# Retention and squared-ReLU feed-forward: two more chunks in halves of 64 tokens, and the preparation for that form placed later

## The chip, the core and the metric

The kernel runs on one core of a Trainium2 chip. A core has TensorE (PE in the profile; its weight loads are PEld), VectorE (DVE), ScalarE (ACT), GpSimd (POOL) and a queue on SyncE (SP) from which this kernel issues all its DMAs. Each engine works through its own instructions in order and waits on semaphores for the others. The metric is device time in microseconds of the whole program. Before the change three runs gave 1238.62, 217.63 and 218.36 us, with 218.36 as the median.

## What is computed

For 4 batches of 8 heads, 768 tokens and 64 dimensions a decaying state is carried along the tokens; the result goes through a feed-forward layer with a squared ReLU.

```python
gamma = 1.0 - 2.0 ** (-5.0 - np.arange(H, dtype=np.float32))
for t in range(S):
    state = gamma[None, :, None, None] * state + np.einsum('bhd,bhe->bhde', k[:, :, t], v[:, :, t])
    y[:, :, t] = scale * np.einsum('bhd,bhde->bhe', q[:, :, t], state)
...
x = np.ascontiguousarray(attn_out.transpose(0, 2, 1, 3)).reshape(B * S, H * D)
h = np.maximum(x @ w_in, 0.0)
return (h * h @ w_out).astype(np.float32)
```

`x` is 3072 x 512, `w_in` 512 x 2048, `w_out` 2048 x 512; all arrays are float32. The kernel multiplies in bf16.

## The kernel before, in words

The tokens are cut into 24 chunks of 128, six to a batch. The decay is taken out by scaling: q is multiplied by a table `qf`, k by a table `kf`, and what is left for a chunk is ordinary masked attention inside it (`scores`: k times q, masked by `cmask` on VectorE; then times v) plus the product of q with the running state of the chunks before it (`state` adds k times v into one PSUM tile, `c_ps`, that lives for a whole batch; `outputs` adds both parts up and ScalarE copies them into `xt`, the feed-forward's input). Heads go in four pairs. A pair is put on the 128 rows of TensorE with zeros where one head's data would meet the other's, hence the block-diagonal tiles `k_bd`, `v_bd` and `s_bd`, whose zero parts are written once.

There are two forms. In the **wide form** (chunks 0 to 11) a chunk is one block of 128 tokens. Its keys are transposed and spread into `k_bd` (`spread_k`, two copies on VectorE, once the transpose is made by DMA), the scores are taken in two portions of two pairs, both through one PSUM tile `st` (`ps_st` has a single buffer), each masked by one instruction at line 394, and the state of a pair is 128 columns wide, of which each head uses its own 64. In the **halves form** (from chunk `PACK_FROM` = 12, functions with a 2 in their names) a chunk is two blocks of 64 tokens, u = 0 and 1, and a row block of 128 holds 64 tokens of each of a pair's two heads. `scale_k2` writes scaled keys block-diagonally (two VectorE instructions of 64 rows), `cast_v2` makes three copies of the values on GpSimd, all of a chunk's scores fit into `st` at once with one masking instruction, the state is renewed after each half (`state2`), and it is only 64 columns wide. This form needs tables and masks of its own (`pack_constants`: memsets and iotas on GpSimd, exponents on VectorE, an exponential on ScalarE) and tiles whose off-diagonal parts are zero (`zero_off_diagonal`, a VectorE memset per half of the tile: `ks_bd2s`, `v_bd2s` and the third of the three `s_bds`).

Loads differ too. A wide chunk's k and v come in one DMA each (`load`). For the halves form `group_loads` fetches three chunks at once, one DMA for each of 8 heads and for k and v, 16 in all, put singly among the other work.

The order of work on every engine is written out by hand. The feed-forward of a block of chunks (`BLOCKS`: 4, then 2 each) is cut into pieces, eight to a chunk, counted from 4 on; a piece is about 0.9 us of TensorE. In blocks 1 and 2 (pieces 33 to 64) eight pieces of the first product of a block's two chunks come before eight of the second. `put(n, f, ...)` places an attention step, a load or a preparation directly after piece n, in the order in which `put` was called; `take_squares` then squares on VectorE (line 584) what ScalarE's ReLU (line 613) has just written. Nothing reorders this afterwards, so a step that must wait holds up all that stands behind it in the same engine's queue.

Places that matter here: the casts of the last quarter of `w_in` after piece 10; scaling of q for chunk 4 after 18 and its transpose on TensorE after 20; `pack_constants` after 8 and the ten zeroing memsets after 10 to 19. For chunk 8 the two portions of scores stand after pieces 50 and 52; for chunk 9 the cast of its values (`v_bd`, waiting until chunk 7's outputs have used the tile) stands after 49, its spread copies after 55, its scores after 57 and 59. A chunk m in the halves form whose outputs stand after piece d has its `scale_k2` and `cast_v2` after d - 15, the DMA transpose of the keys after d - 13, `state2` after d - 6 and d - 3, scores after d - 5. Chunk 10 has d = 70, chunk 11 has 78.

Of the kernel before, what the change touches and what calls it, by code (L numbers as in the profile page):

```python
# [9 lines left out]
FP32 = mybir.dt.float32  # L10
# [3 lines left out]
AF = mybir.ActivationFunctionType  # L14
# [7 lines left out]
DMA_FROM = 8  # L22


PACK_FROM = 12

GROUP = 3


@with_exitstack  # L30
def kernel(
# [9 lines left out]
    nc = tc.nc  # L41
    P = nc.NUM_PARTITIONS

    B, H, S, D = q.shape
    DM, DFF = moe_w_in.shape
    C = 128
    NCH = S // C
    NPAIR = H // 2
# [6 lines left out]
    NCHUNK = len(chunks)  # L55
# [9 lines left out]
    grpool = ctx.enter_context(tc.tile_pool(name="grpool", bufs=2))  # L65
# [13 lines left out]
    ps_c = ctx.enter_context(tc.tile_pool(name="ps_c", bufs=1, space=bass.MemoryType.PSUM))  # L79
# [23 lines left out]
            load_q(m)  # L103
        load_kv(m)

    def group_loads(m):

        b, i = chunks[m]
        for name, src, to in (("kg", k, raw_k), ("vg", v, raw_v)):
            t = grpool.tile([P, 2 * GROUP, NPAIR, D], FP32, name=name)  # L110
            for h in range(H):
                p, hh = divmod(h, 2)
                rows = slice(64 * hh, 64 * (hh + 1))
                nc.sync.dma_start(
                    t[rows, :, p, :],
                    src[b, h, i * C : (i + GROUP) * C, :].rearrange("(w s) d -> s w d", s=64),
                )
                yield
            for j in range(GROUP):
                to[m + j] = t[:, 2 * j : 2 * j + 2].rearrange("s u p d -> s (u p) d")  # L120

    w_in_v = moe_w_in.rearrange("(cb p) f -> p cb f", p=P)
# [28 lines left out]
    halves = [slice(0, 64), slice(64, 128)]  # L151
# [75 lines left out]
    s_bds = [const.tile([P, NPAIR, 2, D], BF16, name=f"s_bd{j}") for j in range(3)]  # L227
    ks_bd2s = [const.tile([P, 2 * NPAIR, 2, D], BF16, name=f"ks_bdp{j}") for j in range(2)]

    v_bd2s = [t.rearrange("s p (c hh) d -> s (p c) hh d", hh=2) for t in v_bds[2:]]  # L230
# [170 lines left out]
    c_ps = [None]  # L401
# [27 lines left out]
    def xt_of(m):  # L429
        tb = block_of[m]  # L430
        if m == first[tb]:
            xts[tb] = xtpool.tile([P, NCB, BLOCKS[tb] * C], BF16, name="xt")
        return tb, (m - first[tb]) * C
# [61 lines left out]
    def half_of(qT, p, u):  # L495
        return qT[:, :, p, u * (C // 4) : (u + 1) * (C // 4)]
# [28 lines left out]
    def state2(m, u):  # L525

        b, i = chunks[m]
        a = at[m]
        if i == NCH - 1 and u == 1:
            return  # L530
        if i == 0 and u == 0:
            c_ps[0] = ps_c.tile([P, NPAIR, D], FP32, name="c_ps")
        c = c_ps[0]
        for p in range(NPAIR):
            nc.tensor.matmul(  # L535
                c[:, p, :],
                lhsT=a["ks"][:, u * NPAIR + p],
                rhs=a["v2"][:, u * NPAIR + p, :],
                start=(i == 0 and u == 0 and p == 0),
                stop=True,  # L540
                skip_group_check=True,
            )
        s_bd = s_bds[(2 * m + u) % 3]
        nc.scalar.activation(s_bd[halves[0], :, 0, :], c[halves[0]], AF.Copy)  # L544
        nc.vector.tensor_copy(s_bd[halves[1], :, 1, :], c[halves[1]])  # L545

    def outputs2(m):
        b, i = chunks[m]
        a = at.pop(m)
        tb, off = xt_of(m)  # L550
        y = ps_y.tile([P, NPAIR, 2, C // 2], FP32, name="y")
        for u in range(2):
            inter = i > 0 or u > 0
            for p in range(NPAIR):
                yv = half_of(y.rearrange("e p r s -> e r p s"), p, u)
                if inter:
                    nc.tensor.matmul(  # L557
                        yv,
                        lhsT=s_bds[(2 * m + u - 1) % 3][:, p],
                        rhs=half_of(a["qT"], p, u),  # L560
                        start=True,
                        stop=False,
                    )
                nc.tensor.matmul(  # L564
                    yv,
                    lhsT=a["v_bd"][:, u * NPAIR + p],
                    rhs=a["pt"][:, u * NPAIR + p, :].rearrange("s (r t) -> s r t", r=2),
                    start=not inter,
                    stop=True,
                )  # L570
        nc.scalar.activation(  # L571
            xts[tb][:, :, off : off + C].rearrange("e p (s r) -> e p r s", r=2),
            y[:],
            AF.Copy,
        )
# [178 lines left out]
    def put(place, what, *args):  # L754
        parts.setdefault(place, []).append((what, args))
# [6 lines left out]
    def attend(m, scaled, places):  # L762
        by_dma = m >= DMA_FROM
        attend_q(m, scaled, scaled if by_dma else places[0])
        put(places[0], scale_kv, m)
        if by_dma:
            put(places[0], dma_transpose_k, m)
        put(places[1], spread_k if by_dma else transpose_k, m)
        put(places[2], scores, m, 0)
        put(places[3], scores, m, 1)  # L770
        put(places[3], state, m)
        put(places[4], outputs, m)

    def attend2(m, d):
        attend_q(m, d - 17, d - 15)
        put(d - 15, scale_k2, m)
        put(d - 15, cast_v2, m)
        put(d - 13, transpose_k2, m)
        put(d - 6, state2, m, 0)
        put(d - 5, scores2, m)  # L780
        put(d - 3, state2, m, 1)
        put(d, outputs2, m)
# [12 lines left out]
    attend(5, None, (27, 29, 31, 33, 35))  # L795
    attend(6, 30, (33, 35, 37, 39, 42))
    attend(7, None, (40, 42, 44, 46, 49))
    put(8, pack_constants)
    for j, t in enumerate(ks_bd2s + v_bd2s):
        for hh in range(2):  # L800
            put(10 + 2 * j + hh, zero_off_diagonal, t, hh)
    for hh in range(2):
        put(18 + hh, zero_off_diagonal, s_bds[2], hh)


    done = [55, 62, 70] + [78 + 8 * j for j in range(13)]
    for m, place in ((8, 26), (9, 31), (10, 36)):
        put(place, load, m)
    for m, d in zip(range(8, NCHUNK), done):
        if m < PACK_FROM:  # L810
            attend(m, d - 15 if d < 70 else d - 16, (d - 13, d - 7, d - 5, d - 3, d))
        else:
            attend2(m, d)
        if m + 3 < PACK_FROM:
            put(d - 13, load, m + 3)
        elif m + 3 < NCHUNK and (m + 3) % 2 == 0:
            put(d - 13, load_q, m + 3)
    for m, place in zip(range(PACK_FROM, NCHUNK, GROUP), (43, 67, 92, 116)):
        loads = group_loads(m)
        for j in range(2 * H):  # L820
            put(place + 3 * j // 2, next, loads)
        put(place + 3 * H, next, loads, None)

    def before(n):
        for what, args in parts.pop(n, []):
# [40 lines left out]
```

## Time and profile before

| what | value |
|---|---|
| median of the three runs | 218.36 us |
| the profiled execution | 219.42 us |
| its span, first to last instruction | 217.65 us |
| mean granted TensorE clock | 1.000 |
| VectorE's squares, line 584 | 96 instructions, 44.0 us |
| zeroing memsets, line 295 | 10 instructions, 2.5 us |
| group loads, line 114 | 64 DMAs of 96 KB, median 2.9 and 2.8 us to landing |
| key transposes by DMA, line 492 | 12, median 3.2 us to landing |

The span lies inside the profiled execution's own time; 1.77 us lie around it. A row of a timeline gives the start in us from the span's start, the time taken, engine, line and operation, what is written from what, and in square brackets how long the engine stood idle before and what ended that. The ends of matmuls are modelled: each shows some 0.2 to 0.4 us although in a stream they start far closer together, so a busy TensorE is not one at its peak, and the spacing of starts says more than the duration.

### The profile page before, as it was taken

What the parts mean: (1) busy time and instruction counts of PE and PEld (TensorE: products, weight loads), DVE (VectorE), ACT (ScalarE), POOL (GpSimd) and SP (SyncE); (2) the same over time, 40 slices, a digit from 0 to 9 for tenths busy, and PEclk for the clock granted to TensorE, in tenths of its full rate; (3) what the DMA queues carried; (4) which work ended last, traced back from release to release, by engine and by line L of the source; (5) the groups of instructions that cost most, each with busy time, mean ns of one, the idle gap of its engine ahead of it and who ended that gap; (6) DMA issues with size and microseconds to landing.
All of it is one profiled execution on the core that took longest, in us unless ns stands there. A gap on an engine that the chain in (4) does not pass through costs nothing.

```text
span 217.7 us, 5060 instructions
## 1 busy us (share of the span) xinstructions
PE 208.9 (96%) x2039; PEld 144.6 (66%) x2039; DVE 132.7 (61%) x257; ACT 119.0 (55%) x219; POOL 48.2 (22%) x103
## 2 busy tenths in 40 slices
PE   6898998899999999999999999999999999999994
PEld 1566743455985895794795785785775875965853
DVE  5766679825566686298379388387396495550420
ACT  8564777346874572472483572581673663753631
POOL 3222763711101110107030331205221223000000
PEclk9999999999999999999999999999999999999999
DMA  6999999998873986569598599697997323301102
GB/s 168 279 257 365 410 375 291 318 258 232 255 181 77 245 206 126 165 170 192 151 210 163 164 232 169 166 204 167 155 217 176 99 50 99 96 3 48 48 3 96
DMA packets 94711, 39.65 MB, mean 182 GB/s; under 512 B 74592, under 2 KB 88160, under 8 KB 94688
## 3 DMA queue, kind: packets, MB, share of 16 engines
q1 hardware_dynamic: 94688, 39.33, 70.3%
q8 instruction: 16, 0.26, 0.5%
q14 instruction: 7, 0.06, 0.1%
HBM read 27.26 MB, written 6.29 MB: 154 GB/s over the span
## 4 chain that ended last, share of the span: by engine, by line
PE 82%; DVE 11%; ACT 3%; DMA 2%; issue 1%; DVEq 0%; ACTq 0%
PE psf L662 35%; PE psf L604 33%; DVE h L584 3%; DVE qs L300 2%; PE y L450 2%; PE st L387 2%; DMA qn<-in_q_dram 2%; PE st L508 1%; PE y L564 1%; PE y L557 1%; PE c_ps L535 1%; PE tp L333 1%; ACT h L613 1%; PE c_ps L413 1%; DVE pt L394 1%
## 5 line engine op out<-in xcount | busy, mean ns | idle before, releaser
L604 PE MATMUL psf<-xt,w_in_bf 128*128 128x256 bf16 (+2 forms) x880 | 91.4, 259 | 1.0 <-DVE w_in_bf L259 0.6
L662 PE MATMUL psf<-w_out_bf,h 128*128 128x512 bf16 (+2 forms) x400 | 89.8, 371 | 0.0
L604 PEld LDWEIGHTS <-w_in_bf 128*128 128x128 bf16 x880 | 71.5, 98 | 13.2 <-DVE w_in_bf L259 1.4
L613 ACT ACTIVATE h<-psf 128x512 bf16<-128x512 f32 x96 | 56.8, 596 | 23.0 <-PE psf L604 20.4
L662 PEld LDWEIGHTS <-h 128*128 128x128 bf16 x400 | 36.3, 98 | 34.9
L584 DVE TENSOR_TENSOR h<-h 128x512 bf16<-128x512 bf16 x96 | 44.0, 471 | 21.8 <-ACT h L613 20.8
L672 ACT ACTIVATE osb<-psf 128x512 f32<-128x512 f32 (+2 forms) x25 | 14.4, 580 | 27.1 <-PE psf L662 26.9
L545 DVE CAST s_bd<-c_ps 64x256 bf16<-64x256 f32 x22 | 9.4, 428 | 27.0 <-ACT s_bd L544 26.5
L394 DVE TENSOR_TENSOR pt<-st,cmask 128x512 bf16<-128x512 f32 x20 | 13.8, 692 | 18.4 <-PE st L387 18.1
L483 POOL CAST v<-vg 128x512 bf16<-128x512 f32 x12 | 7.7, 643 | 55.8 <-PE c_ps L535 22.5
L319 POOL CAST v_bd<-vn 128x512 bf16<-128x512 f32 x12 | 8.1, 671 | 52.2 <-PE y L450 33.0
L486 POOL CAST v_bd<-vg 64x512 bf16<-64x512 f32 x24 | 15.9, 662 | 16.6 <-PE y L564 15.9
L470 DVE TENSOR_TENSOR ks_bdp<-kg,kf 64x512 bf16<-64x512 f32 x24 | 18.4, 765 | 0.4
L300 DVE TENSOR_TENSOR qs<-qn,qf 128x1024 bf16<-128x1024 f32 x12 | 14.9, 1240 | 0.8 <-DMA qn<-in_q_dram 0.8
L571 ACT ACTIVATE xt<-y 128x512 bf16<-128x512 f32 x12 | 8.9, 743 | 9.6 <-PE y L564 9.6
L458 ACT ACTIVATE xt<-y 128x512 bf16<-128x512 f32 x12 | 9.0, 749 | 7.9 <-PE y L450 7.5
L544 ACT ACTIVATE s_bd<-c_ps 64x256 bf16<-64x256 f32 x22 | 8.1, 367 | 8.8 <-PE c_ps L535 8.8
L279 PE MATMUL psf<-ident 128*128 128x512 bf16 (+1 forms) x48 | 8.9, 328 | 2.1 <-POOL ident L178 2.1
L387 PEld LDWEIGHTS <-k_bd 128*128 128x128 bf16 x96 | 6.7, 98 | 4.5 <-ACT k_bd L353 1.2
L267 POOL CAST w_out_bf<-w_stage 128x512 bf16<-128x512 f32 x12 | 8.5, 746 | 5.2 <-DMA w_stage<-in_moe_w_out_dram 5.2
L353 ACT ACTIVATE k_bd<-tp 64x512 bf16<-64x512 bf16 x12 | 7.1, 588 | 4.6 <-PE tp L346 4.5
L450 PE MATMUL y<-pt,v_bd 128*128 128x128 bf16 x96 | 9.2, 219 | 0.0
(67 smaller groups left out, 162.7 us busy)
## 6 DMA issues: line engine op xcount, KB each, us to landing
qn<-in_q_dram SPq DMA_DIRECT2D x12, 512.0 KB, 4.9
out_dram<-osb SPq DMA_DIRECT2D x23, 256.0 KB, 2.2
w_stage<-in_moe_w_out_dram SPq DMA_DIRECT2D x4, 1024.0 KB, 9.3
kn<-in_k_dram SPq DMA_DIRECT2D x12, 256.0 KB, 4.7
vn<-in_v_dram SPq DMA_DIRECT2D x12, 256.0 KB, 4.6
w_stage<-in_moe_w_in_dram SPq DMA_DIRECT2D x3, 1024.0 KB, 10.3
kg<-in_k_dram SPq DMA_DIRECT2D x32, 96.0 KB, 2.9
vg<-in_v_dram SPq DMA_DIRECT2D x32, 96.0 KB, 2.8
```

What stands on the lines that cost most here:

```text
L300: nc.vector.tensor_tensor(out=qs[:], in0=raw_q.pop(m).rearrange("s h r d -> s r h d"), in1=qf[:, i : i + 2, :, None].to_broadcast([P, 2, H ...
L387: nc.tensor.matmul(st[:, pp, hh, :], lhsT=a["k_bd"][:, p, hh, :], rhs=a["qT"][:, :, p, :], start=True, stop=True,)
L394: nc.vector.tensor_tensor(out=a["pt"][:, 2 * half : 2 * half + 2], in0=st[:], in1=cmask.rearrange("s r t -> s (r t)")[:, None, None, :].to ...
L450: nc.tensor.matmul(y[:, p, :], lhsT=a["v_bd"][:, p, 2 * hh : 2 * hh + 2, :], rhs=a["pt"][:, p, hh, :], start=(i == 0 and hh == 0), stop=(h ...
L470: nc.vector.tensor_tensor(out=ks[rows, :, hh, :], in0=kn[rows], in1=kf2[rows, i].rearrange("s u p -> s (u p)")[:, :, None].to_broadcast([6 ...
L486: nc.gpsimd.tensor_copy(v_bd[rows, :, hh, :], vn[rows])
L545: nc.vector.tensor_copy(s_bd[halves[1], :, 1, :], c[halves[1]])
L584: nc.vector.tensor_mul(hv, hv, hv)
L604: nc.tensor.matmul(hp, lhsT=w_in_bf[g][:, cb, fq * 128 : (fq + 1) * 128], rhs=xts[tb][:, cb, cols], start=(cb == 0), stop=(cb == NCB - 1),)
L613: nc.scalar.activation(hv, hp[:], AF.Relu)
L662: nc.tensor.matmul(op[:], lhsT=h_of(tb, f)[:, 0, j * C : (j + 1) * C], rhs=w_out_bf[g][:, fq, cols], start=(f == 0), stop=(f == NFB - 1),)
L672: nc.scalar.activation(osb[:, cols], op[:], AF.Copy)
```

## The change

Chunks 10 and 11, the last two of the second batch, move to the halves form (`PACK_FROM` 10). Their batch began in the wide form, so its running state stays wide for them: `state2` multiplies with the block-diagonal `v_bd` to 128 columns, takes the second heads' part from where the wide form has it, and the first half of chunk 10 reads the state tile that `state` left after chunk 9 (`last_state`). From chunk 12 on the state is narrow as it was, but lies in a PSUM tile of the wide layout. Groups now have sizes 2, 3, 3, 3, 3; the first, for chunks 10 and 11, starts after piece 35 and replaces their single loads of k and v. `pack_constants` moves from piece 8 to 50, and the ten memsets from pieces 10 to 19 to pieces 51 to 64, beginning with `s_bds[2]`.

```diff
-PACK_FROM = 12
-GROUP = 3
+PACK_FROM = 10
+GROUPS = [2, 3, 3, 3, 3]
...
-    def group_loads(m):
+    def group_loads(m, size):
...
-            t = grpool.tile([P, 2 * GROUP, NPAIR, D], FP32, name=name)
+            t = grpool.tile([P, 2 * max(GROUPS), NPAIR, D], FP32, name=name)
...
+        wide = m - i < PACK_FROM
         if i == 0 and u == 0:
-            c_ps[0] = ps_c.tile([P, NPAIR, D], FP32, name="c_ps")
+            c_ps[0] = ps_c.tile([P, NPAIR, 2, D], FP32, name="c_ps")
         c = c_ps[0]
         for p in range(NPAIR):
             nc.tensor.matmul(
-                c[:, p, :],
+                c[:, p] if wide else c[:, p, 0, :],
                 lhsT=a["ks"][:, u * NPAIR + p],
-                rhs=a["v2"][:, u * NPAIR + p, :],
+                rhs=a["v_bd"][:, u * NPAIR + p] if wide else a["v2"][:, u * NPAIR + p, :],
...
-        nc.scalar.activation(s_bd[halves[0], :, 0, :], c[halves[0]], AF.Copy)
-        nc.vector.tensor_copy(s_bd[halves[1], :, 1, :], c[halves[1]])
+        second = 1 if wide else 0
+        nc.scalar.activation(s_bd[halves[0], :, 0, :], c[halves[0], :, 0, :], AF.Copy)
+        nc.vector.tensor_copy(s_bd[halves[1], :, 1, :], c[halves[1], :, second, :])
+
+    def last_state(m, u):
+        if u == 0 and m == PACK_FROM:
+            return s_bds[(m - 1) % 2]
+        return s_bds[(2 * m + u - 1) % 3]
...
-                        lhsT=s_bds[(2 * m + u - 1) % 3][:, p],
+                        lhsT=last_state(m, u)[:, p],
...
-    put(8, pack_constants)
-    for j, t in enumerate(ks_bd2s + v_bd2s):
+    put(50, pack_constants)
+    for j, t in enumerate([s_bds[2]] + ks_bd2s + v_bd2s):
         for hh in range(2):
-            put(10 + 2 * j + hh, zero_off_diagonal, t, hh)
-    for hh in range(2):
-        put(18 + hh, zero_off_diagonal, s_bds[2], hh)
+            put(51 + 3 * j + hh, zero_off_diagonal, t, hh)
...
-    for m, place in ((8, 26), (9, 31), (10, 36)):
-        put(place, load, m)
+    put(26, load, 8)
+    put(31, load, 9)
+    put(36, load_q, 10)
...
-    for m, place in zip(range(PACK_FROM, NCHUNK, GROUP), (43, 67, 92, 116)):
-        loads = group_loads(m)
+    m = PACK_FROM
+    for size, place in zip(GROUPS, (35, 43, 67, 92, 116)):
+        loads = group_loads(m, size)
         for j in range(2 * H):
-            put(place + 3 * j // 2, next, loads)
-        put(place + 3 * H, next, loads, None)
+            put(place + (9 if size == 2 else 12) * j // 8, next, loads)
+        put(place + (18 if size == 2 else 24), next, loads, None)
+        m += size
```

More of the change, by code (lines that the diff above doesn't have):

```diff
@@ L114, in group_loads @@
                 nc.sync.dma_start(
-                    t[rows, :, p, :],
-                    src[b, h, i * C : (i + GROUP) * C, :].rearrange("(w s) d -> s w d", s=64),
+                    t[rows, 0 : 2 * size, p, :],
+                    src[b, h, i * C : (i + size) * C, :].rearrange("(w s) d -> s w d", s=64),
                 )
                 yield
-            for j in range(GROUP):
+            for j in range(size):
                 to[m + j] = t[:, 2 * j : 2 * j + 2].rearrange("s u p d -> s (u p) d")
```

## The prediction

> **What bounds the kernel now.** I read the page's busy table and chain first.
>
> ```profile
> PE 208.9 (96%) x2039; PEld 144.6 (66%) x2039; DVE 132.7 (61%) x257; ACT 119.0 (55%) x219; POOL 48.2 (22%) x103
> ...
> PE 82%; DVE 11%; ACT 3%; DMA 2%; issue 1%; DVEq 0%; ACTq 0%
> ```
>
> PE carries 82% of the chain, so only fewer PE columns or fewer PE waits can shorten the span. Next, the timeline of PE: every row with an idle time after 26 us.
>
> ```profile
> 33.76 0.39 PE L604 MATMUL psf<-xt,w_in_bf 128*128 128x512 bf16 x1 [0.36 <-DVE w_in_bf L259]
> 34.37 3.41 PE L604 MATMUL psf<-xt,w_in_bf 128*128 128x512 bf16 x15 [0.22 <-DVE w_in_bf L259]
> ...
> 41.94 0.62 PE L333 MATMUL tp<-ident,qs 128*128 128x128 bf16 x8 [0.70 <-DVE qs L300]
> ```
>
> ```profile
> 101.32 0.38 PE L387 MATMUL st<-qT,k_bd 128*128 128x128 bf16 x4 [0.17 <-DVE pt L394]
> ```
>
> The bracket counts from the modelled end of the matmul before (0.38 us), but 512-column matmuls in a stream start 0.216 us apart (x8 in 1.73 us in the chain). Each bracket hides 0.16 us more, so the losses are 0.52, 0.40, 0.87 and 0.33 us, 2.12 in all. Nothing else stops PE from 26 us to the end. All four name DVE. What DVE did before the first three:
>
> ```profile
> 30.51 0.59 DVE L158 CAST ex_k_f<-ex_k_i 128x48 f32<-128x48 int32 x1
> 31.14 0.54 DVE L159 TENSOR_TENSOR ex_k_f<-ex_k_f,lng 128x48 f32<-128x48 f32 x1
> ...
> 33.00 1.71 DVE L259 CAST w_in_bf<-w_stage 128x256 bf16<-128x256 f32 x4
> 34.71 0.27 DVE L295 MEMSET ks_bdp<- 64x256 uint32 x1
> ```
>
> The tables' exponents stand ahead of the weight casts; from 34.71 on eight memsets, one between every two squares, stand ahead of the scaled queries (40.65 to 41.88). Both are moved. Where they go, DVE and POOL look like this (DVE, then POOL there, then POOL at the tables' present place, then PE):
>
> ```profile
> 75.33 0.69 DVE L394 TENSOR_TENSOR pt<-st,cmask 128x512 bf16<-128x512 f32 x1 [0.73 <-PE st L387]
> ...
> 82.89 0.69 DVE L394 TENSOR_TENSOR pt<-st,cmask 128x512 bf16<-128x512 f32 x1
> ```
>
> ```profile
> 74.30 0.77 POOL L319 CAST v_bd<-vn 128x512 bf16<-128x512 f32 x1 [6.91 <-PE y L450]
> ```
>
> ```profile
> 25.32 0.41 POOL L207 MEMSET lng<- 64x2 f32 x8
> 25.79 0.59 POOL L156 IOTA ex_k_i<- 64x48 int32 x2
> ```
>
> ```profile
> 76.91 0.39 PE L387 MATMUL st<-qT,k_bd 128*128 128x128 bf16 x4
> ...
> 84.42 0.39 PE L387 MATMUL st<-qT,k_bd 128*128 128x128 bf16 x4
> ```
>
> PE reaches the second half of chunk 8's scores at 76.91 and of chunk 9's at 84.42. ps_st has one buffer, so each waits for DVE's mask product (L394) of the first half. Now it ends 0.9 and 0.8 us ahead.
>
> **Part 1: early places emptied.** Without the exponents ScalarE no longer waits 1.1 us for them (its table exponential at 31.71), so the relu after piece 9 can follow PE's end at 30.81 and runs to 31.45, DVE squares it to 31.9 and the four casts start at 31.9, not 33.00. Even at the slow 0.69 us each (beside POOL casts) the first two end at 32.7 and 33.4; PE wants them at 33.24 and 33.45. Gone: 0.92. Without memsets DVE follows the relus, the last square ends near 37.9 (PE 0.92 earlier), the scaled queries at 39.1 to 39.4; PE comes for them at 40.15. Gone: 0.87. I looked at what is next late: the loads for chunks 4 to 9 landed 3 us or more ahead of their use, the last two w_out groups are cast 3 us ahead. So 1.79 saved.
>
> **Part 2: PE columns.** Spacing at 128 columns is 0.056 us (four L387 from 74.90, next row 75.12); at 64, 0.029:
>
> ```profile
> 107.52 0.40 PE L508 MATMUL st<-qT,kT 128*128 128x64 bf16 x8
> 107.75 1.47 PE L604 MATMUL psf<-xt,w_in_bf 128*128 128x256 bf16 x12
> ```
>
> Chunk 10 now: 8 scores, 4 state, 12 outputs, 24 x 0.056 = 1.344. In halves: 8 + 16 at 0.029, and the state as 8 at 0.056 since it stays wide: 1.144. Chunk 11, without a state after its second half: 20 x 0.056 = 1.12 to 24 x 0.029 + 4 x 0.056 = 0.92. Saved 0.40. The stall at 101.32 is between the two score halves of chunk 11; in halves of 64 there is one mask product per chunk and no second fill of st, and chunks 12 to 23 in that form show no such stall. Saved 0.33. The strided narrow c_ps costs nothing that PE waits for: the wide state's eviction takes 375 ns, the narrow one's 367.
>
> **Part 3: the new places.** At piece 50 the tables stand on POOL behind the cast for chunk 9, which waits for chunk 7's outputs (74.30 to 75.07 above). Eight memsets and two iotas take 1.06 (25.32 to 26.38): 76.13. On DVE the exponents wait for that at the head of an in-order queue, with chunk 8's first mask product (ready 75.33) right behind. They take 0.51 (the same pair at the kernel's start, 1.80 to 2.31) to 1.09 (30.51 to 31.60, POOL casting beside them); POOL will do memsets as at the start, so 0.51. The mask product runs 76.64 to 77.33; PE, due at 76.91, stalls 0.47. DVE then has no pause up to chunk 9's first mask product. Before, that stretch (75.33 to 82.89) was 7.56 with 0.88 of waiting: 6.68 of work. Added: two memsets of s_bds[2], 0.43; three of ks_bd2s, 0.70; scale_k2 of chunk 10, put ahead of that mask product, 1.44 (97.62 to 99.06). Taken away: 0.30, as no POOL cast now lies beside the second spread copy (0.59 against 0.29). Sum 8.95, so it starts at 85.59, ends 86.28, and PE goes on at 86.33, not 84.42: **1.91 lost**, the 0.47 within it. Behind it, four more memsets and scale_k2 of chunk 11 (2.5 us) lie beside second products that need no square, and DVE has caught up by 90.4; from piece 65 on the order is that of chunks 12 to 23.
>
> Bounds: 1.5 where memsets take only their 0.20 spacing and squares fill gaps; 3.3 where the exponents take 1.09 and POOL's three new casts for chunk 10 meet scale_k2 (its rows are 0.69 alone, 1.12 beside a POOL cast, twice 0.43). Those casts wait for the values' last group load and probably come later, so I stay at 1.91. The Trainium skill, "SBUF — State Buffer", section "SBUF: two separate sides", says that GpSimd and a VectorE instruction with two SBUF inputs hold a shared port pair exclusively for a whole instruction. By it each scale_k2 could lose a whole cast (0.66) rather than 0.43, and by that estimate the upper bound would be 3.8.
>
> SP: sixteen group loads for chunks 10 and 11 at about 0.62 each replace four loads at 0.57; eleven stand behind chunk 8's query transpose. SP was already behind there (chunk 9's key transpose was issued at 75.25, its keys were scaled by 73.80). I count it 2.7 later against PE, landing 2.6 to 4.4 after issue, at 80.6 to 82.3 on before's clock. DVE reaches the spread copy at 82.4: covered, barely.
>
> **Sum.** 1.79 + 0.40 + 0.33 - 1.91 = 0.61 saved: span 217.65 to 217.0. The profiled execution took 219.42, 1.77 around its span and 1.06 over the median of 218.36; on the median 0.6 less is 217.7.
>
> **Rivals.** *DVE's queue at 76 to 86 us is covered*: for it, DVE is 61% busy overall, and squares may slide back without harm; against it, the mask product is in order behind everything counted. Then 2.5 saved: 215.8. Chance 0.13.
>
> *SP delays chunk 9's keys* (slower side): if the issue costs 1.23 (one group-load row) for two loads and the transpose takes 5 us, it lands near 84, DVE idles 1.6 and scores and all behind move with it: 1.91 becomes 3.5, so 0.9 slower, 219.3. It decides from a landing past 82.4; for it the thin cover, against it that SP starts the first group loads in idle time before chunk 8's queries are scaled. Chance 0.20.
>
> *Halves save no PE time*: were each 64-column matmul held to 0.056 by its own weight load, 32 and 28 of them would cost 0.45 more per chunk, 0.90 lost in place of 0.40 saved: 219.0. The 0.23 for eight above excludes it nearly; chance 0.02. The Trainium skill, "TensorE: Matmul & The Clock Gate", section "Back-to-back issue gap", holds that in a stream of weight load and matmul both set the spacing, 81 ns at 128 columns; by that estimate 16 more matmuls would cost 1.3 us. The trace disagrees, 56 and 29 ns.
>
> **Numbers.** My forecast has 0.60, with 217.3 to 219.1 by its bounds (1.5 lost saves 1.0, 3.3 lost costs 0.8); 0.05 stays for what I don't see. The range of 8 in 10 reaches 215.8 to 219.3. A difference under 2% (4.4 us) is about what a measurement can't tell from no change. More gain than 2.5 isn't there to be had, and 4.4 lost needs several delays: faster 0.01, within 0.97, slower 0.02.
>
> **What would show it.** Right: PE without idle before L604 near 33 us and L333 near 40; a PE wait for L394 of 0.3 to 1 us near 75.6 and of 1 to 1.7 near 83 to 84.5, with DVE busy without pause ahead of each and the exponents released by POOL; none near 99. Wrong: no PE wait for L394 there (first rival), or a DVE wait for kT before the copy of line 376 near 81 that PE inherits (second). The sum is wrong above all if the score waits differ from 1.9.

## The result and the profile after

The change made the kernel slower by a little: 219.34 us median against 218.66 (22 runs each), ratio 1.0037 [1.0019, 1.0054]. Two repeats of the same pair gave 1.0019 [0.9994, 1.0044] and 1.0010 [0.9982, 1.0039], whose intervals include no change. So it costs 0.2 to 0.8 us by the three ratios, where 0.6 us of gain was forecast. The profiled executions taken alone say something else: span 217.2 after, 217.65 before.

The busy table and the chain of waits of the kernel after:

```profile
PE 208.2 (96%) x2055; PEld 144.2 (66%) x2055; DVE 131.3 (60%) x255; ACT 119.6 (55%) x221; POOL 51.6 (24%) x107
...
PE 86%; DVE 6%; DMA 3%; ACT 2%; issue 1%; POOL 1%; DVEq 0%; ACTq 0%; POOLq 0%
```

VectorE's part of the chain fell from 11% to 6%; DMA has 3% (2% before), and GpSimd 1%, which is new. The timeline of PE in the stretches that the prediction named (start, time, engine, line, operation, tiles, shapes, count, and in brackets the idle time before and its releaser):

```profile
25.82 11.14 PE L613 MATMUL psf<-xt,w_in_bf 128*128 128x128 bf16 x59
...
40.25 0.61 PE L333 MATMUL tp<-ident,qs 128*128 128x128 bf16 x8
...
75.52 0.38 PE L387 MATMUL st<-qT,k_bd 128*128 128x128 bf16 x4
...
81.07 0.66 PE L387 MATMUL st<-qT,k_bd 128*128 128x128 bf16 x4
...
84.61 0.38 PE L387 MATMUL st<-qT,k_bd 128*128 128x128 bf16 x4 [1.14 <-DVE pt L394]
...
99.26 0.40 PE L508 MATMUL st<-qT,kT 128*128 128x64 bf16 x8
```

In kernels with the halves form from chunk 10 on, the lines behind `state2` stand 9 further down: L593, L613, L622 and L671 there are L584, L604, L613 and L662 of the kernel before.

The first products of the first block run as one row, and the transposes of the queries at 40.25 have no bracket: the early stalls are gone. None stands before 99.26 either. In their place PE stands before chunk 9's second portion at 84.61; with the 0.16 us that a bracket hides after a 512-column matmul that is 1.31. Where the model of the ends hides a wait entirely, the distance of starts shows it: 0.31 lost before the row at 75.52, and 0.27 inside the row at 81.07, whose four matmuls take 0.66 where they take 0.39. In sum 1.88. What VectorE did there:

```profile
74.28 0.22 DVE L158 CAST ex_k_f<-ex_k_i 128x48 f32<-128x48 int32 x1 [0.76 <-POOL ex_k_i L156]
74.54 0.21 DVE L159 TENSOR_TENSOR ex_k_f<-ex_k_f,lng 128x48 f32<-128x48 f32 x1
74.78 0.69 DVE L394 TENSOR_TENSOR pt<-st,cmask 128x512 bf16<-128x512 f32 x1
...
80.73 0.61 DVE L376 COPY k_bd<-kT 64x512 bf16<-64x512 bf16 x2 [0.27 <-DMA kT<-ks]
81.37 1.40 DVE L470 TENSOR_TENSOR ks_bdp<-kg,kf 64x512 bf16<-64x512 f32 x2
82.81 0.76 DVE L593 TENSOR_TENSOR h<-h 128x512 bf16<-128x512 bf16 x2
83.56 0.27 DVE L295 MEMSET ks_bdp<- 64x256 uint32 x1
83.86 0.69 DVE L394 TENSOR_TENSOR pt<-st,cmask 128x512 bf16<-128x512 f32 x1
```

The exponents wait for GpSimd with the first mask product behind them, and `scale_k2` (L470, 1.40 us) stands ahead of the second, as forecast. One row was forecast the other way: the spread copies wait 0.27 us for the DMA transpose of chunk 9's keys.

### The profile page after: what moved, and what is told of

It is laid out like the page before. It is cut to its first block, busy times and chain, and to the rows that moved or that the text cites. A ratio compares the mean times of both kernels' runs of the same rounds, so it can differ in the third digit from the quotient of the medians.

```text
span 217.2 us, 5108 instructions
## 1 busy us (share of the span) xinstructions
PE 208.2 (96%) x2055; PEld 144.2 (66%) x2055; DVE 131.3 (60%) x255; ACT 119.6 (55%) x221; POOL 51.6 (24%) x107
## 4 chain that ended last, share of the span: by engine, by line
PE 86%; DVE 6%; DMA 3%; ACT 2%; issue 1%; POOL 1%; DVEq 0%; ACTq 0%; POOLq 0%
PE psf L671 37%; PE psf L613 36%; DMA qn<-in_q_dram 2%; PE y L450 2%; DVE pt L394 2%; PE st L508 2%; PE y L573 1%; PE c_ps L538 1%; PE y L566 1%; PE st L387 1%; DMA kT<-ks 1%; DVE qs L300 1%; PE tp L333 1%; PE c_ps L413 1%; PE tp L346 1%
## 5 line engine op out<-in xcount | busy, mean ns | idle before, releaser
L613 PE MATMUL psf<-xt,w_in_bf 128*128 128x256 bf16 (+2 forms) x880 | 91.1, 259 | 0.4 <-ACT xt L458 0.4
L671 PE MATMUL psf<-w_out_bf,h 128*128 128x512 bf16 (+2 forms) x400 | 89.6, 371 | 0.0
L613 PEld LDWEIGHTS <-w_in_bf 128*128 128x128 bf16 x880 | 71.5, 98 | 12.0 <-issue 0.7
L622 ACT ACTIVATE h<-psf 128x512 bf16<-128x512 f32 x96 | 56.9, 596 | 22.0 <-PE psf L613 19.4
L671 PEld LDWEIGHTS <-h 128*128 128x128 bf16 x400 | 36.3, 98 | 35.0
L593 DVE TENSOR_TENSOR h<-h 128x512 bf16<-128x512 bf16 x96 | 43.8, 471 | 21.3 <-ACT h L622 20.5
L549 DVE CAST s_bd<-c_ps 64x256 bf16<-64x256 f32 x25 | 10.7, 428 | 31.4 <-ACT s_bd L548 31.1
L483 POOL CAST v<-vg 128x512 bf16<-128x512 f32 x14 | 9.4, 673 | 62.7 <-DMA kg<-in_k_dram 19.2
L486 POOL CAST v_bd<-vg 64x512 bf16<-64x512 f32 x28 | 19.2, 685 | 18.1 <-PE y L573 17.3
L470 DVE TENSOR_TENSOR ks_bdp<-kg,kf 64x512 bf16<-64x512 f32 x28 | 20.9, 748 | 0.5
L394 DVE TENSOR_TENSOR pt<-st,cmask 128x512 bf16<-128x512 f32 x16 | 11.1, 691 | 14.2 <-PE st L387 13.9
L319 POOL CAST v_bd<-vn 128x512 bf16<-128x512 f32 x10 | 7.0, 695 | 38.2 <-DMA vn<-in_v_dram 19.5
L548 ACT ACTIVATE s_bd<-c_ps 64x256 bf16<-64x256 f32 x25 | 9.2, 366 | 8.8 <-PE c_ps L538 8.8
L515 DVE TENSOR_TENSOR pt<-st,cmask 128x512 bf16<-128x512 f32 x14 | 9.7, 692 | 0.5
L425 ACT ACTIVATE s_bd<-c_ps 64x256 bf16<-64x256 f32 x13 | 4.9, 376 | 8.3 <-PE c_ps L413 8.1
L267 POOL CAST w_out_bf<-w_stage 128x512 bf16<-128x512 f32 x12 | 7.9, 697 | 5.6 <-DMA w_stage<-in_moe_w_out_dram 5.6
```

The source lines that it names most:

```text
L394: nc.vector.tensor_tensor(out=a["pt"][:, 2 * half : 2 * half + 2], in0=st[:], in1=cmask.rearrange("s r t -> s (r t)")[:, None, None, :].to ...
L470: nc.vector.tensor_tensor(out=ks[rows, :, hh, :], in0=kn[rows], in1=kf2[rows, i].rearrange("s u p -> s (u p)")[:, :, None].to_broadcast([6 ...
L486: nc.gpsimd.tensor_copy(v_bd[rows, :, hh, :], vn[rows])
L515: nc.vector.tensor_tensor(out=pt[:], in0=st[:], in1=cmask2.rearrange("s r t -> s (r t)")[:, None, :].to_broadcast([P, 2 * NPAIR, C // 2]), ...
L549: nc.vector.tensor_copy(s_bd[halves[1], :, 1, :], c[halves[1], :, second, :])
L593: nc.vector.tensor_mul(hv, hv, hv)
```

## The accounts of all profiles

PE's time can be split without a model: the start of the first 512-column matmul of the feed-forward (its last wait is for ScalarE's copy into `xt`; nothing that the change moves releases it), the losses after it (each start-to-start distance beyond the one in a stream, summed), and the rest of the span.

| kernel | ratio to before | start | lost before 45 us | lost 45 to 92 | lost near 100 | rest |
|---|---|---|---|---|---|---|
| before | | 26.33 | 1.78 | 0.04 | 0.33 | 189.16 |
| before_again | 0.9992 [0.9961, 1.0024] | 26.21 | 0.19 | 0.04 | 0.32 | 189.14 |
| before_third | 0.9992 [0.9965, 1.0019] | 26.93 | 0.77 | 0.04 | 0.32 | 189.16 |
| before_fourth | 1.0010 [0.9984, 1.0036] | 27.00 | 2.13 | 0.05 | 0.31 | 189.17 |
| after | 1.0037 [1.0019, 1.0054] | 26.44 | 0 | 1.92 | 0 | 188.80 |
| after_again | 1.0019 [0.9994, 1.0044] | 26.17 | 0 | 2.23 | 0 | 188.81 |
| after_third | 1.0010 [0.9982, 1.0039] | 26.28 | 0 | 1.88 | 0 | 188.80 |
| moves_only | 0.9973 [0.9946, 0.9999] | 26.30 | 0 | 0.48 | 0.31 | 189.16 |
| halves_only | 1.0026 [0.9998, 1.0055] | 26.41 | 1.04 | 2.19 | 0 | 188.82 |
| loads_early | 1.0066 [1.0041, 1.0092] | 26.95 | 0 | 3.21 | 0 | 188.79 |
| k2_late | 1.0159 [1.0126, 1.0193] | 25.90 | 0 | 2.83 | 0 | 188.81 |
| prep_early | 1.0001 [0.9982, 1.0020] | 26.25 | 0 | 2.01 | 0 | 188.80 |
| all_three | 0.9961 [0.9931, 0.9990] | 26.98 | 0 | 0.10 | 0 | 188.80 |
| all_three_again | 0.9949 [0.9924, 0.9974] | 25.94 | 0 | 1.94 | 0 | 188.80 |
| halves_mended | 0.9996 [0.9971, 1.0020] | 27.18 | 0.09 | 0.71 | 0 | 188.81 |
| prep_only | 0.9927 [0.9905, 0.9949] | 25.88 | 0 | 0.04 | 0.31 | 189.13 |
| prep_only_again | 0.9961 [0.9939, 0.9983] | 26.06 | 0 | 0.04 | 0.31 | 189.14 |

The ratios are not quotients of the medians, from which they differ by up to 0.0015. The rest has two values, 189.15 in the old form and 188.80 in the new, equal within 0.04 over all profiles. Everything that differs between two executions of one kernel is in the start (26.2 to 27.0 in before, 25.9 to 27.2 over all kernels) and in the losses.

## The experiments

**The two kernels again.** A second profile of each; times beside the same runs of before as the next two experiments.

> The kernel before once more, for a second profile and for the noise. Theory A (the profiled execution of before is typical; what the change removes is in every execution): PE loses about 0.9 us to the weight casts near 33 us, 0.9 us to the scaled queries near 41 us and 0.3 us near 100 us, as in the first profile. Theory B (the first profile of before, 0.8 us over its median, shows early losses that many executions don't have, since they hang on when loads land and which POOL casts then lie beside VectorE's): the early losses differ by 0.5 us or more from the 1.79 us of the first profile, and the span with them. Timed ratio 1.000 within 0.003 by both.

> The changed kernel once more. Both theories: no PE loss at 33 and 41 us; PE loses 1.9 us in all (1.6 to 2.3) at chunk 8's and chunk 9's second score portions, with VectorE busy without pause before. Theory A: ratio to before 0.995 to 0.999. Theory B: ratio 1.002 to 1.005, as the 22 runs had it.

Before lost 0.19 us early, not 1.79. After lost 2.2 late again. A stall that was taken for a fixed part of the kernel is thus not always there. The timeline of before_again (GpSimd's row between those of VectorE):

```profile
30.23 0.17 DVE L158 CAST ex_k_f<-ex_k_i 128x48 f32<-128x48 int32 x1
30.44 0.21 DVE L159 TENSOR_TENSOR ex_k_f<-ex_k_f,lng 128x48 f32<-128x48 f32 x1
...
30.84 1.92 POOL L267 CAST w_out_bf<-w_stage 128x512 bf16<-128x512 f32 x3 [1.34 <-DMA w_stage<-in_moe_w_out_dram]
...
32.21 1.30 DVE L259 CAST w_in_bf<-w_stage 128x256 bf16<-128x256 f32 x4
```

In the first profile of before GpSimd cast `w_out` from 29.70 on and the two exponents, at 30.51, took 0.59 and 0.54 us. Here the first `w_out` load landed at 30.78 instead of 29.64, the casts came after the exponents, and these took 0.17 and 0.21. The casts of `w_in` begin 0.8 us earlier, and PE finds them in time.

**Each half of the change alone.** moves_only keeps the halves form from chunk 12 on and moves the preparation only:

```diff
-    put(8, pack_constants)
-    for j, t in enumerate(ks_bd2s + v_bd2s):
+    put(50, pack_constants)
+    for j, t in enumerate([s_bds[2]] + ks_bd2s + v_bd2s):
         for hh in range(2):
-            put(10 + 2 * j + hh, zero_off_diagonal, t, hh)
-    for hh in range(2):
-        put(18 + hh, zero_off_diagonal, s_bds[2], hh)
+            put(51 + 3 * j + hh, zero_off_diagonal, t, hh)
```

halves_only has the halves form from chunk 10 on, with the preparation left where it was.

> Only the tables and memsets moved, chunks 10 and 11 in the wide form. Both theories: no PE loss at 33 and 41 us; the first score wait (chunk 8) 0.3 to 0.5 us as in the changed kernel, the second (chunk 9) 0.3 to 0.5 us in place of 1.6, since scale_k2 of chunk 10 (1.44 us) isn't ahead of the mask product; the 0.33 us near 99 us is back. Theory A: 0.9 us faster than before, ratio 0.996. Theory B (typical early losses under 1.2 us): ratio 0.998 to 1.002.

> Chunks 10 and 11 in halves, tables and memsets left after pieces 8 to 19. Both theories: the early losses as in before; no wait for the tables at piece 50; PE waits 0.2 to 0.6 us for chunk 9's first mask product behind scale_k2, none near 99 us; packing saves 0.40 us. So 0.2 to 0.6 us faster than before in both, ratio 0.997 to 0.999. If it is slower than before, something in the halves form costs that neither theory has (the group loads on SP, the later landing of chunk 9's keys).

moves_only: 0.9973 [0.9946, 0.9999], 0.6 us faster. It lost 0.43 at the tables' new place and nothing at chunk 9. halves_only: 1.0026 [0.9998, 1.0055]. The preparation is early there, so nothing of it stands in VectorE's queue, and yet 2.19 us are lost between 72 and 86. Its timeline says by what:

```profile
79.15 1.73 SPq L367 DMA_TRANSPOSE kT<-ks  x1
...
82.30 0.61 DVE L376 COPY k_bd<-kT 64x512 bf16<-64x512 bf16 x2 [2.21 <-DMA kT<-ks]
...
82.64 0.66 PE L387 MATMUL st<-qT,k_bd 128*128 128x128 bf16 x4 [0.68 <-DVE k_bd L376]
85.92 0.27 PE L387 MATMUL st<-qT,k_bd 128*128 128x128 bf16 x2 [0.88 <-DVE pt L394]
```

VectorE stands idle for 2.21 us until the keys of chunk 9 are transposed; SP issues that transpose at 79.15, behind the group loads. So the second rival of the prediction is real: where VectorE is on time, SP is not. The second wait, before 85.92, is not SP's alone, since `scale_k2` (1.41 us) still stands between the late copies and the mask product.

**One suspect at a time, and all of them.** Four kernels, each after with one edit: the group loads for chunks 10 and 11 earlier (loads_early), `scale_k2` of chunk 10 two pieces later, with its casts (k2_late), the preparation at pieces 21 to 30, where a second product runs and no square is due (prep_early), and the three together (all_three).

```diff
-            put(place + (9 if size == 2 else 12) * j // 8, next, loads)
+            put(32 + j // 2 if size == 2 else place + 12 * j // 8, next, loads)
```

```diff
-        put(d - 15, scale_k2, m)
-        put(d - 15, cast_v2, m)
-        put(d - 13, transpose_k2, m)
+        late = 2 if m == PACK_FROM else 0
+        put(d - 15 + late, scale_k2, m)
+        put(d - 15 + late, cast_v2, m)
+        put(d - 13 + late // 2, transpose_k2, m)
```

```diff
-    put(50, pack_constants)
+    put(30, pack_constants)
...
-            put(51 + 3 * j + hh, zero_off_diagonal, t, hh)
+            put(21 + 2 * j + hh, zero_off_diagonal, t, hh)
```

> The changed kernel with the group loads of chunks 10 and 11 after pieces 32 to 39, two to a piece, ahead of the waits on SP. Theory Q (VectorE's queue sets the loss: tables, memsets, scale_k2, all ahead of chunk 9's first mask product): the key transpose of chunk 9 is issued some 3 us earlier, VectorE doesn't wait for it, but the two score waits still sum to 1.5 to 1.9 us; ratio to before about 1.000. Theory S (SP's queue sets it, the key transpose behind eleven loads): the second wait falls below 0.8, the sum to about 1 us; ratio 0.996.

> The changed kernel with scale_k2 and cast_v2 of chunk 10 after piece 57, behind chunk 9's first mask product, and its key transpose after 58. Theory Q: the second wait falls by 1.44 us from 1.57 to 0.1 to 0.4, the sum to 0.5 to 0.9; ratio 0.996 to 0.998. Theory S: VectorE is held by the late transpose of chunk 9's keys, the second wait stays above 0.7. Rival to both: chunk 10's own keys come late and PE waits at its scores after piece 65 in exchange.

> The changed kernel with the tables after piece 30 and the memsets after pieces 21 to 30, where a block's second product needs no squares. Theory Q: no wait at chunk 8's second portion, and the second wait shrinks by the tables and memsets (about 1.9 us of VectorE's work gone), to under 0.3; ratio about 0.993. Theory S, with what the run with halves only showed: VectorE stands idle for chunk 9's keys, and the waits still sum to 1.5 to 2.2; ratio 1.000 to 1.003. Both: no loss at 33 and 41 us, and none where the preparation now stands.

> Loads early, scale_k2 late and preparation early together. Both theories: no PE wait for the score tile at chunks 8 and 9 and none near 33, 41 and 99 us; what the profile of PE then shows as lost after 26 us is under 0.3 us, the span 215.0 to 215.4, the ratio to before 0.990 to 0.994 (early losses of before being about 1.0 us on average in three profiles, with 0.40 for packing and 0.33 for the last wait). If the ratio is above 0.996, something else is lost that the profiles haven't shown.

No single edit helps. loads_early is slower still, 1.0066 [1.0041, 1.0092]. The transpose of chunk 9's keys now lands in time (79.99), but the loads landed early too, and GpSimd's casts of the values moved up beside VectorE's work:

```profile
76.63 1.56 POOL L486 CAST v_bd<-vg 64x512 bf16<-64x512 f32 x2
78.25 0.61 POOL L483 CAST v<-vg 128x512 bf16<-128x512 f32 x1
78.81 1.36 POOL L486 CAST v_bd<-vg 64x512 bf16<-64x512 f32 x2
...
79.62 1.63 DVE L300 TENSOR_TENSOR qs<-qn,qf 128x1024 bf16<-128x1024 f32 x1
...
82.53 0.61 DVE L376 COPY k_bd<-kT 64x512 bf16<-64x512 bf16 x2
```

The scaled queries took 1.63 us, 1.22 in after; the copies have no bracket, so it is VectorE that is late now at chunk 9, not SP.

k2_late takes the second wait away as the theory says (0.03 left at chunk 9), so `scale_k2` ahead of the mask product was the larger part of it. But PE then waits for chunk 10's own keys. Their transpose stands at the same place in SP's queue as in after, behind the same group loads, and is issued only 0.96 us earlier (86.65 against 87.61), while PE comes for the scores 2.0 us earlier (89.18 against 91.14); it also took 4.8 us to land, 3.2 in after:

```profile
86.65 1.28 SPq L492 DMA_TRANSPOSE kT<-ks_bdp  x1
...
91.50 0.41 PE L508 MATMUL st<-qT,kT 128*128 128x64 bf16 x8 [2.16 <-DMA kT<-ks_bdp]
```

Its profiled execution took 219.3, the median 221.92; what its other executions lost beyond that no profile shows. prep_early is level with before, 1.0001 [0.9982, 1.0020]. VectorE is free early, and waits for the same transpose as in halves_only:

```profile
80.90 0.61 DVE L376 COPY k_bd<-kT 64x512 bf16<-64x512 bf16 x2 [2.04 <-DMA kT<-ks]
```

All three together lost 0.10 us in this profile: 0.9961 [0.9931, 0.9990]. The losses are as forecast, the ratio is not: 0.990 to 0.994 was expected, and 0.9961 lies just above the limit from which something else is lost. The second profile of this kernel, below, shows what that can be.

**Is it the halves form or the moved preparation that pays?** prep_only is the kernel before with the preparation at pieces 21 to 30 and nothing else changed; before, after and all_three ran beside it.

> The kernel before with nothing changed but the places of the preparation: tables after piece 30, memsets after 21 to 30. Its gain is the early loss by itself. Theory A (1.79 us in every execution): 1.8 us faster, ratio 0.992. Theory B (about 1.0 us on average, from 0.2 to 1.8 by the landing of the loads): ratio 0.994 to 0.997. Profile by both: no loss at 33 and 41 us, no wait for the tables, the 0.33 us near 99 us still there.

> A third profile of the kernel before. Theory A: early losses 1.6 to 1.9 us. Theory B: anywhere from 0.2 to 1.8, small where the first w_out load lands late against TensorE's arrival at the second quarter (so that POOL's casts lie behind VectorE's exponents, not beside them) and large where it lands early.

> A third profile of the changed kernel. Both: score waits 1.9 to 2.4 us in all, none at 33 and 41 us. Ratio 1.001 to 1.004 by theory B with an early loss of 1.0 on average: 2.1 lost, 1.0 + 0.40 + 0.33 gained.

> The version with all three placements mended, on another chip or hour: no waits, ratio 0.990 to 0.997. Theory B says 0.40 + 0.33 better than with the preparation moved alone, so 0.9965 less than that run's ratio in the same call; if the two are equal, the halves form itself brings nothing.

prep_only had the lowest ratio of all, 0.9927 [0.9905, 0.9949]. The timeline of VectorE shows what it removed: no exponents before the casts of `w_in`, no memsets before the scaled queries.

```profile
31.03 0.87 DVE L584 TENSOR_TENSOR h<-h 128x512 bf16<-128x512 bf16 x1 [0.44 <-ACT h L613]
31.82 1.71 DVE L259 CAST w_in_bf<-w_stage 128x256 bf16<-128x256 f32 x4
...
37.41 1.22 DVE L300 TENSOR_TENSOR qs<-qn,qf 128x1024 bf16<-128x1024 f32 x1
```

all_three_again: 0.9949 [0.9924, 0.9974], not to be told apart from prep_only, although the halves form has 0.67 less to do (0.35 of columns, 0.32 near 100). Its profile gives them back:

```profile
56.18 5.63 SPq L114 DMA_DIRECT2D kg<-in_k_dram  x8
61.91 0.55 SPq L91 DMA_DIRECT2D qn<-in_q_dram  x1
62.50 6.29 SPq L114 DMA_DIRECT2D vg<-in_v_dram  x8
68.91 1.33 SPq L359 DMA_TRANSPOSE qT<-qs  x1
...
72.68 1.35 DVE L376 COPY k_bd<-kT 64x512 bf16<-64x512 bf16 x2 [3.03 <-DMA kT<-ks]
```

Chunk 8's queries were scaled by 64.4; SP issues their transpose at 68.91, because sixteen group loads take 11.9 us to issue ahead of it. VectorE waits 3.03 us for the keys behind, and PE loses 1.9. The profile of all_three, the same kernel, has nearly the same times on the clock:

```profile
68.41 1.70 SPq L359 DMA_TRANSPOSE qT<-qs  x1
...
72.56 0.61 DVE L376 COPY k_bd<-kT 64x512 bf16<-64x512 bf16 x2 [1.86 <-DMA kT<-ks]
```

Its first stage, however, had ended 1.04 us later (26.98 against 25.94), so PE came later too and lost only 0.10. In these two executions the keys of chunk 8 came when SP's queue let them, and what the earlier start had gained was lost again in waiting.

**The group loads out of the way, and the early stalls once more.** halves_mended is all_three with its sixteen loads one per piece after pieces 24 to 39.

```diff
-            put(32 + j // 2 if size == 2 else place + 12 * j // 8, next, loads)
+            put(24 + j if size == 2 else place + 12 * j // 8, next, loads)
```

> all_three with its sixteen group loads for chunks 10 and 11 put one per piece after pieces 24 to 39, so that all are issued before SyncE comes to chunk 8's query transpose. Theory (the late waits of the change came from two queues, VectorE's and SyncE's, and the halves form itself saves what its 64-column matmuls and the missing last wait are worth, 0.66 us): no TensorE loss after 26 us above 0.5 in sum, and a time 0.4 to 0.8 us below prep_only_again, ratio to before 0.989 to 0.992. Rival (the sixteen DMAs cost more elsewhere, whatever their place, so the form brings nothing here): the time is equal to or above prep_only_again's, with losses in the profile between 44 and 92 us of 0.6 or more, or with a first stage longer than 27 us.

> The kernel before with only the preparation moved to pieces 21 to 30, a second time. If the early stalls of before cost 1.6 us on average: ratio 0.991 to 0.994. If they cost 0.9, the mean of the three profiles of before: ratio 0.995 to 0.997.

> The kernel before again: ratio 1.000 within 0.002. Its profile is a fourth look at the early stalls: 1.79, 0.19 and 0.77 us so far. If the size goes with when the weights land, the first L604 of 512 columns near 26.3 or later goes with a loss of 0.8 or more only if VectorE's exponents run beside GpSimd's w_out casts (0.5 us each instead of 0.2).

halves_mended: 0.9996 [0.9971, 1.0020], against 0.9961 [0.9939, 0.9983] for prep_only_again. Its premise failed: SP issues almost without a pause from 43.7 to 72 us, so the spread loads end as late as before, and chunk 8 still waits.

```profile
65.52 2.57 SPq L114 DMA_DIRECT2D vg<-in_v_dram  x4
68.20 2.61 SPq L359 DMA_TRANSPOSE qT<-qs  x1
...
73.27 0.93 DVE L376 COPY k_bd<-kT 64x512 bf16<-64x512 bf16 x2 [2.28 <-DMA kT<-ks]
```

In prep_only_again SP has nothing to issue from 60.3 to 64.56 and issues that transpose at 64.56. So what the form costs is room in SP's queue, sixteen issues of 0.62 to 0.79 us on average in place of four. Nor are the start and this loss independent. Chunk 8's keys landed 45.6 us after the start in all_three (0.10 lost), 46.1 in halves_mended (0.71) and 46.7 in all_three_again (1.94); on the clock these landings are 72.53, 73.25 and 72.66. halves_mended's profiled execution, 218.56, is typical of it (median 218.53) and has the longest start of all, 27.18. By the signs set beforehand the rival came out: a median 0.92 above prep_only_again's, 0.71 us lost between 44 and 92, a start above 27.

before_fourth had the largest early loss, 2.13. Its timeline is the other case of before_again:

```profile
30.54 1.93 POOL L267 CAST w_out_bf<-w_stage 128x512 bf16<-128x512 f32 x3 [1.16 <-DMA w_stage<-in_moe_w_out_dram]
...
31.35 0.59 DVE L158 CAST ex_k_f<-ex_k_i 128x48 f32<-128x48 int32 x1
31.98 0.54 DVE L159 TENSOR_TENSOR ex_k_f<-ex_k_f,lng 128x48 f32<-128x48 f32 x1
...
33.87 1.71 DVE L259 CAST w_in_bf<-w_stage 128x256 bf16<-128x256 f32 x4
...
34.63 0.39 PE L604 MATMUL psf<-xt,w_in_bf 128*128 128x512 bf16 x1 [0.55 <-DVE w_in_bf L259]
```

The load landed nearly as late as in before_again (30.49), but this execution's start was late too (27.00 against 26.21). What fits the profiles is not the landing alone but the landing against the compute: 3.5 us after the start here, 3.3 in the first profile, 4.6 in before_again. In before_third it was 2.7: there GpSimd's casts had ended when the second exponent ran, which took 0.21, and the early loss was 0.77. halves_only, whose early places are those of before, adds a fifth: 3.9 us, exponents of 0.60 and 0.54, 1.04 lost. No run set the landing on purpose, so this stays an argument from five profiles.

## Why the prediction was wrong, point by point

**The early places (1.79 saved): mechanism right, size wrong; this is the step that failed.** The profiled execution of before held a stall of 1.79 us, and "So 1.79 saved" was taken from every execution. Four profiles of before lost 1.78, 0.19, 0.77 and 2.13, 1.22 on average. prep_only, which removes just this, says the same by times: 0.73% and 0.39% of 218.76 are 1.6 and 0.85 us, and the medians differ by 1.34 and 1.15; both give 1.2 on average. The text even held the hint: the profiled execution was 1.06 above the median, and the forecast subtracted from the median a stall that was 0.56 larger than the average one.

**The columns (0.40) and the last wait (0.33): right.** 189.15 became 188.80, 0.35 saved; 0.32 near 100 us is gone. The rival that halves save no PE time is excluded. The Trainium skill, "TensorE: Matmul & The Clock Gate", section "Back-to-back issue gap", would have had the 16 more matmuls cost 1.3 us, by an estimate from its 81 ns each; the measurement disagrees and decides.

**The new places (1.91 lost): right in size, one cause short.** Three profiles of after lost 1.92, 2.23 and 1.88 between 45 and 92 us. The tables' wait was 0.31 to 0.43 (0.47 forecast), chunk 9's second portion took most of the rest, and k2_late shows that `scale_k2` carries much of it. But the key transpose, "covered, barely", was not always: VectorE waited 0.27 and 0.34 us for it in two of the three profiles. In after_third it landed just as VectorE came (80.51, the copies at 80.53), and 1.88 were lost all the same, so VectorE's queue makes this loss by itself, as forecast. The rival that put SP's price at 1.6 more was wrong for the change as made, since VectorE's delay and SP's run side by side and only the longer counts; that its 219.3 lies beside the measured 219.34 is chance. halves_only and prep_early, where VectorE is early, show SP's delay: 2.2 and 2.0 us of VectorE's idle time. That is also why VectorE's part could not be won back alone.

**The upper bound's mechanism** (GpSimd's casts beside chunk 10's `scale_k2`) did not occur in after, where it took 1.40 us; chunk 11's took 1.68 beside the casts, with nothing waiting for it. In loads_early, where the casts come early, they met the scaled queries instead: 0.41 more. The Trainium skill, "SBUF — State Buffer", section "SBUF: two separate sides", lets a VectorE instruction with two SBUF inputs wait for a whole GpSimd instruction; the second exponent of before, which has two, agrees in that it took 0.33 longer beside casts of 0.64 each, less than one of them.

**The sum.** With the sizes measured: 1.22 + 0.35 + 0.32 = 1.89 saved, 1.97 lost (the mean of the three, 2.01, less 0.04 that before has in the same stretch too): 0.1 us slower, nearly nothing, where the three ratios have 0.2 to 0.8 us lost. Of the 1.6 us between the forecast of 217.7 and the measured 219.34, 0.3 is the base (218.36 was the median of three runs, 218.66 that of 22), 0.57 the early places, and 0.12 the other three terms together; 0.6 is left. The choice of executions may account for it: the profiled ones of after were 0.24 us faster than the medians of their runs on average (218.93, 218.98 and 218.73 against 219.34, 219.20 and 218.82), the four of before 0.30 slower (219.42, 217.66, 219.01 and 220.46 against 218.66, 218.93, 218.78 and 218.98). With both set right the account would have after 0.6 us slower, an estimate that lies inside the three ratios. In which stage the executions without a profile differ isn't shown and stays open.

**What was gained in the end.** The moving of the preparation pays by itself: 0.6 us at the place that the change chose (moves_only, 0.9973 [0.9946, 0.9999]), 0.4 to 0.7% at pieces 21 to 30 (prep_only). The halves form for chunks 10 and 11 has 0.67 us less to do in every profile, but no run shows that gain in the time: all_three and all_three_again aren't told apart from prep_only, and halves_mended is slower than prep_only_again. That it would come with room in SP's queue is argued from the profiles; a form that fetches the two chunks in fewer, larger DMAs was not tried. The Trainium skill, "DMA: Bandwidth & Descriptors", section "Rules for kernel authors", advises to coalesce small transfers; the rows here agree as far as SP goes: a group load for two chunks (64 KB) takes 0.62 us to issue near 75 us in after, a chunk's load of 256 KB 0.57 near 69 us in before.

## What to carry to other kernels

A stall read from one profile is a sample: if the profiled execution is above the median, some of the stall may be what put it there, so look at a second profile before subtracting it, and compare the profiled executions of both kernels with the medians of their runs. When work moves into a stretch, price each queue that it lengthens by itself, since two queues late by the same amount hide each other and removing one shows nothing. And test preparation that is moved together with a new form without the form: here that part alone was the gain.

## What the hardware showed unexpectedly

Two short VectorE instructions took 0.17 and 0.21 us or 0.59 and 0.54, with the same operands, by whether GpSimd was casting beside them; ScalarE's exponential, its relu, VectorE's square and the `w_in` casts follow behind them, and the early losses ranged from 0.19 to 2.13 us. The first stage took 26.2 to 27.0 us in four executions of before, and 25.9 to 27.2 over all kernels. And an issue on SP took about the same time for 64 KB as for 256 KB where it went fast (0.62 and 0.57 us; up to 2.3 and 2.9 elsewhere), so a finer cut of the same loads can fill a queue that had room before.
